# Tail scores of two heads moved from one full-array product into four quarter-array products, output weights rounded on chip, new order of work

## The chip, the cores and the metric

One core of a Trainium2 chip runs the whole program. The metric is device time in microseconds of one execution, as a median of runs; less is better. TensorE (PE, with its weight loads listed apart as PEld), VectorE (DVE), ScalarE (ACT) and GpSimd (POOL) compute, and the queue of SyncE (SP) issues nearly all DMAs.

## The reference

Two stages. First an attention with a window of 128 keys and a linear bias per head, over 8 batches, 8 heads, 576 positions, head size 64:

```python
scores = scale * q @ k.T
mask = (rel >= 0) & (rel < 128)
attn = softmax(where(mask, scores + bias, -1e9)); x = attn @ v
```

Then four experts of causal attention on x (8 x 576 x 512), the two best experts of each position weighted by their gate:

```python
w, topk = softmax of the 2 largest of x @ w_gate
for e in range(4):
    q, k, v = x @ wq[e], x @ wk[e], x @ wv[e]
    ye = causal_softmax(scale * q @ k.T) @ v @ wo[e]
    out += (weight of e in topk, else 0) * ye
```

## The kernel before

Two heads of a batch form a pair `g` (32 pairs, four in each batch). In SBUF the 64 dimensions of head 0 lie in partitions 0 to 63 and those of head 1 in 64 to 127. The 576 query rows of a head are four blocks of 128 and a tail of 64 rows. A block needs the keys of its own block and of the one ahead, the tail the last 192 keys.

Scores of the blocks (`products`) are fp32 products of 64x64 weights: each quarter of the PE array takes 64 rows of one head against 128 or 192 keys, and four such products, one in each quarter, stand together. `attn_s(g, 0)` makes blocks 0 and 1 of both heads (a group of four with 128 columns and one with 192), `attn_s(g, 1)` blocks 2 and 3 (two groups with 192). The tails of the two heads are the unit `attn_s(g, 2)`: one product over the whole array, whose 128x128 weights hold head 0's tail and zeros above, zeros and head 1's tail below, against 192 key columns, into a PSUM bank of its own. An fp32 product shows as two matmul records. Then DVE folds the late keys over the early ones (`copy_predicated`), adds the bias and takes the maximum, and ACT takes the exponential.

Inputs of a pair come in one SBUF slot `r` of the pool `big5`: `load` issues two DMAs of 288 KB (and the one of V), `load_hi` one of 64 KB with the tail's weights. `big5` has nine slots of 1280 floats; pairs' inputs, their probabilities, the experts' V and probabilities, and the raw weights share them. The first batch's four pairs go by another path (`half_s`, `half_tail`), with their own loads.

The output weights `wo` are needed rounded (`WOH`) and as a remainder (`WOL`). Before, `WOH` comes by a converting DMA that POOL issues, and POOL makes `WOL` from it and from the raw copy, which SP's queue loads.

Everything is recorded first, then issued in an order written out as a packed string (`ORDER`): each engine executes its instructions in that order, and SP's queue its DMAs. `plan` keeps the products of a quarter group together. Slots of a pool are given out along that order, the longest free first, so a load waits until the slot's last user is done. All instructions are issued by one line (L1185).

Of the kernel before, what the change touches and what calls it, by code (L numbers as in the profile page):

```python
# [34 lines left out]
K = {'nb': 0, 'm0': 8, 'm1': 0, 'he': 3, 'kj': 1, 'ot': 2, 'rn': 1, 'gr': 0, 'pw': 0.9, 'wa2': 0.9, 'q0': 0.1, 'q1': 1.0, 'wc': 3, 'se': 0, 'hd': 1, 'S': 2, 'T': 2, 'A': 2, 'X': 1, 'M': 1, 'apv': 0, 'alag': 2, 'vorder': 0, 'na': 1, 'pp': 3, 'tp': 6, 'mp': 3, 'ta0': 0.08, 'ta1': 0.91, 'sa0': 0.1, 'sa1': 1.0, 'sb0': 0.68, 'sb1': 0.77, 'tb0': -0.03, 'tb1': 1.08, 'wo0': 0.1, 'wo1': 0.45, 'wa0': 0.05, 'wa1': 1.3, 'aa0': 0.0, 'aa1': 1.04, 'ab0': -0.04, 'ab1': 1.0, 'xp': 5, 'ts': 1, 'lead': 0, 'na0': 2, 'wb0': 0.18, 'wb1': 1.0, 'sh': 0, 'man': 1, 'mode': 'rank', 'chn': 150, 'wu': 0, 'w0': 0.04, 'w1': 0.83, 'w3': 1.15, 'wd': 2}  # L35
# [7 lines left out]
    "b)oif*-BkgVLWqaFtT{ZkYf#(NCy06W%5K-#fYof}o*n4^`S<XhW%!bsPa1OM`AnL-(9}1W{_DSlTzz7$z8B<II(BY0qyt|HMgYT!%a9*#&*m*@yir6K"
    "Lr**f!ZR;Js7@N)4jsb-a8wM$yuLvgyw{zZ9(K8tOUH`~LUj{-X)2`Qc|>sJWm+A!wUmo;Z)xJ*cCoY6J!MO>nZT*dwSl)-_^|Cyr+GbSxF<jQ$LA|zn"
    "y9xZHo+pmt!<|jO2O+X*H!ZADFD*|cZp;8viPjLl>9;-(w+6WMPSAk*KT|7=v+BrAqzX&>wWTT<^CF9wI=TA&pn<dSel@*rLhIPdu;&zy=8z@|M7>!&Q"
    "Cj2>Y&vLTiUjc)&>Y#;RFUyXUCKQY>)(cy-w$blQQt!12{f{5O$IuuNBAs(I1M9UGMvJy*9%%b%AHoXF#Kl2cbbo<u(4w640b!2Vh?zfXOlZ$Z!{aGlB"
    "_+igy$ww?MshvTx9q|55(^TA{=gOam)MNom_xUl_}D4-PTU7n+4iVG^K)qClt7)m8g3s@k9Z&EGs~aBuw6<D$M^0KUPVrnl~%<`3GMfAL;^=#D4B?Q**"
    "o0P62eLN4&L&2E^_GU-iv2#(r9N0lKP#$b`Z+7E_OWBEmGjbCe=Ek?Dg%Y`nax>aEaR(Y#=zhH!)eFf~We6l>)x8j045|a+_1v1C8j27Z?6S<O<IyXNj"
    "7{j6U=IQzFEO5Z$0UQ#KWI{C=aPvpM{`Wte`{7lc2I+N1>&~d|(`?blKD@r}y&-DtX){7W+lZE5U|v{lZHfCu<LcziPF-Gp=()JM7W-to{XhTY`B!s-e"
    "6dNizxN><!v4_U?X5#j9=HH9^{INR!{x3XaYD=I9?2~7)Y-AyD*(L1Yu!S965pKyMx=+uRr`0pEoR*r61+Q}WP>L=v3;1LjN}e1ul8-O;s4HbXS&vqkv"  # L50
    "cnN>;@<(ZZ^^}8Tc;`Ix~6<7x5c40lvIsmCsH;Xh}@q+cWH@4iJQ^AKRUM{pIuN#&sAlJaWBLKMI|%{AuYFw9y%QCVTb81z&sd!~b;%b{cWk<ES<l(p%"
    "-kS}@?hUE|^1)wA4ha|UCN^CQpH1o_c{-o-8LxZtwg(maverhz8~bZ7tJB*FgNBzQ}vNBD}fb62s82dDM#f57~a4xxu?zLDk3;LUe(Nj|3`{OOiCVAAU"
# [20 lines left out]
    "1Fg1qJl%avzH;`n-de}r0{gDq`H2H<CKCn3rSc$E|V!-YaR{aoY#J$Os*D{?mJ%+b|{Q^ahZy4+grD;nHO|Fhmkgw1+&5LudX+FMmbX-=4#Zbx7`n*Yh"
    "5g)9v?wSn+d<IS$ScCMv>RqGd;l25nL~kJ`)V|sC#)jH9zCAFMRdW+6i%@pGj`<3ln-ZpGp})rt0VwY2M|DNG8K{{more;f0VArpd~v6z<rGf8|8U;=&"
    "B}XOWH&e>&`>)&g@c~IX*t<_^h>o3H`nz*wu7(20xjAw!p4E-=-S8AS3WB|eK4?f4WXSMj;%MgkBy!KKZcfOr-O?vsZCeEno(9dcDn<P92<3;cl`1Fw%"
    "mD7=J990l6FveL!3K@lN$>&sW`f3Ya@tQ3pBtf+}<^~ySFvGCAT+t8-~b|+_#g{@&T*=(f%x_p#6gn_64+P6D&yY0PU$YN66MJkU))K>cENB`O}wng>Y"
    "kKm$-fljPLq<%e{^^Ta9Z-$Py0ujWVnCROBaNA7Bss9aKZq;~%VkELbatPjPh)Ro$IVyuI5uNa|vsx?V?v9S?Ol7wQgD2e{Yq<3{%kJo54|<Ywj$XA-8"
# [1195 lines left out]
```

## Time and profile before

| | |
|---|---|
| time, median of 3 runs | 510.36 us (509.54 to 511.25) |
| profiled execution | 512.19 us, its span 510.4 us |
| granted PE clock | 0.997 of full speed |
| PE busy | 499.9 us (98%), 5044 matmuls |
| DVE, ACT, POOL busy | 418.6, 357.5, 171.6 us |
| DMA | 44.87 MB, mean 88 GB/s |

Times are in us unless marked ns. The span runs from the first to the last instruction of the profiled execution. Matmuls are pipelined, so durations of neighbouring matmuls overlap: the price of one in a stream is the distance from its start to the next one's, not its own duration.

### The profile page before, as it was taken

Reading aid. Unit: us, or ns where it says so; the run is one execution under the profiler, and the core shown is the slowest. Engines: PE = TensorE matmul, PEld = TensorE weight load, DVE = VectorE, ACT = ScalarE, POOL = GpSimd, SP = SyncE. Lnnn points to the kernel's source line nnn. Section 1 sums busy time; section 2 is a strip of 40 time slices with the busy share of each in tenths; the row PEclk is TensorE's granted clock in tenths of the full one; section 3 lists DMA queues with packets and bytes.
Section 4 is the critical chain, followed back from the end, with each engine's and each line's share of the span. In section 5 each row is a group of like instructions: output and inputs, shape, how many; then the busy total and the mean of one; then the engine's idle time right before and its main releaser. Section 6 shows DMA issues by size and latency. Waiting matters only on the chain.

```text
span 510.4 us, 14576 instructions
## 1 busy us (share of the span) xinstructions
PE 499.9 (98%) x5044; PEld 429.2 (84%) x5044; DVE 418.6 (82%) x1875; ACT 357.5 (70%) x1338; POOL 171.6 (34%) x382
## 2 busy tenths in 40 slices
...
GB/s 202 283 200 201 50 117 70 3 53 156 19 134 99 2 28 230 6 193 17 19 186 59 103 2 91 193 1 3 150 92 128 99 2 1 91 22 1 1 83 125
DMA packets 27307, 44.87 MB, mean 88 GB/s; under 512 B 3169, under 2 KB 11361, under 8 KB 27233
## 3 DMA queue, kind: packets, MB, share of 16 engines
q1 hardware_dynamic: 26352, 42.95, 31.2%
...
q10 hardware_dynamic: 736, 0.46, 0.3%
q0 software_dynamic: 144, 0.52, 0.3%
...
## 4 chain that ended last, share of the span: by engine, by line
PE 95%; DMA 3%; DVE 1%; ACT 0%; issue 0%; SPq 0%
PE ps L1185 95%; DMA w<-in_hd 3%; DVE w L1185 0%; ACT w L1185 0%; DVE ps L1185 0%; DVE r L1185 0%; DVE ps L1183 0%; DVE nmA L1185 0%; SPq L1185 0%
## 5 line engine op out<-in xcount | busy, mean ns | idle before, releaser
L1185 PE MATMUL ps<-wx,WH 128*128 128x288 f32 (+2 forms) x512 | 113.0, 301 | 0.0
L1185 ACT ACTIVATE w<-w,nm 128x128 f32<-128x128 f32 x252 | 98.6, 394 | 20.1 <-DVE nm L1185 19.9
L1185 POOL TENSOR_SCALAR w<-w,mr,w 128x256 f32<-128x256 f32 (+3 forms) x128 | 76.4, 607 | 91.2 <-DVE r L1185 28.7
L1185 ACT COPY w<-ps 128x512 f32<-128x512 f32 (+3 forms) x144 | 67.2, 491 | 38.4 <-PE ps L1185 28.7
L1185 POOL TENSOR_SCALAR w<-w,r 128x128 f32<-128x128 f32 x141 | 50.5, 370 | 121.9 <-DVE r L1185 89.0
L1185 PEld LDWEIGHTS ps<-wx,WH 128*128 128x128 f32 x512 | 83.8, 189 | 1.6 <-DVE mnm L1185 0.3
L1185 ACT ACTIVATE w<-w,mnm 128x128 f32<-128x128 f32 (+3 forms) x128 | 70.7, 554 | 18.5 <-DVE mnm L1185 18.4
L1185 PE MATMUL ps<-idt,w 128*128 128x128 f32 x608 | 80.3, 275 | 2.0 <-DVE nmA L1185 2.0
L1185 DVE CUSTOM_DVE_ANT_0 w<-ps,tbt 128x128 f32<-128x128 f32 x288 | 73.1, 284 | 4.8 <-PE ps L1185 2.6
L1185 PEld LDWEIGHTS ps<-idt,w 128*128 128x128 f32 x608 | 68.8, 141 | 7.0 <-ACT w L1185 2.7
L1185 DVE TENSOR_TENSOR w<-ps,tmt 128x512 f32<-128x512 f32 (+2 forms) x96 | 71.6, 771 | 3.6 <-ACT w L1185 2.1
L1185 PE MATMUL ps<-wx,WL 128*128 128x288 f32 (+2 forms) x256 | 72.0, 297 | 0.0
L1185 PE MATMUL ps<-w 64*64 64x192 f32 (+2 forms) x1088 | 63.2, 321 | 3.3 <-DMA w<-in_hd 3.3
L1185 PE MATMUL ps<-w,vt 128*64 128x256 f32 (+2 forms) x784 | 65.8, 308 | 0.0
L1185 PE MATMUL ps<-WH,wx 128*128 128x260 f32 x288 | 63.7, 289 | 0.0
L1185 PEld LDWEIGHTS ps<-w,vt 128*64 128x64 f32 x784 | 44.8, 137 | 19.6 <-issue 3.0
L1185 ACT ACTIVATE w<-w,r 128x128 f32<-128x128 f32 x147 | 52.1, 395 | 7.8 <-DVE r L1185 7.3
L1185 DVE COPY w<-ps 128x512 f32<-128x512 f32 (+3 forms) x78 | 43.1, 558 | 17.1 <-PE ps L1185 16.7
L1185 PEld LDWEIGHTS ps<-w 64*64 64x64 f32 (+1 forms) x1088 | 45.1, 139 | 13.7 <-issue 4.2
L1185 DVE COPY_PREDICATED ps<-mkt,ps 128x128 f32<-128x128 int32 (+2 forms) x160 | 50.0, 329 | 7.0 <-PE ps L1185 6.0
L1185 PE MATMUL ps<-w,w 128*64 128x64 f32 (+4 forms) x576 | 53.2, 319 | 0.0
L1185 DVE CUSTOM_DVE_ANT_0 w<-ps,mtt 128x384 f32<-128x384 f32 (+2 forms) x96 | 50.5, 550 | 1.7 <-PE ps L1185 1.3
...
## 6 DMA issues: line engine op xcount, KB each, us to landing
w<-in_hd SPq DMA_DIRECT2D x56, 288.0 KB, 5.1
...
```

The source lines that it names most:

```text
L1185: getattr(getattr(tc.nc, e), m)(*a, **k)
```

## The change

For the 28 pairs of the later batches, the tail's single product goes and four products take its place, one in each quarter, right behind the groups of `attn_s(g, 0)`: head 0's tail against key block 3 (128 columns), head 1's tail against key block 3 (128 columns), and each against the last 64 keys (64 columns). They write free columns of the two PSUM banks of that unit, and the tail's bias and exponential follow there; the unit `attn_s(g, 2)` is empty. The lower half of the array now needs head 1's tail and keys too, so `load_hi` issues three DMAs (32 KB in pieces of 256 bytes, 32 KB in pieces of 512, 16 KB in pieces of 256) in place of one of 64 KB, and the slots of `big5` grow to 1344 floats and fall from nine to eight; the pool `big2` has ten slots in place of nine. `WOH` is no longer loaded by the converting DMA: it is rounded from the raw copy by POOL or ACT. The order string is another: unpacked it has 5851 entries in place of 5795, 16 filler matmuls as before.

```diff
-K = {... 'wd': 2}
+K = {... 'wd': 0}
 ORDER = (
...
-    pp = big5 = _Slots(cp, 9, 10 * P, "w5")
+    pp = big5 = _Slots(cp, 8, 2 * S + 3 * D, "w5")
     tp = big10 = _Slots(cp, 4, 2 * (S + TAIL + S), "w10")
-    big2 = _Slots(cp, 9, DM, "w2")
+    big2 = _Slots(cp, 10, DM, "w2")
...
     def load(g):
-        r = big5.tile([P, 2 * S + P], F32, tag="r", name=f"r{g}")
+        r = big5.tile([P, 2 * S + 3 * D], F32, tag="r", name=f"r{g}")
...
     def load_hi(g):
         b, p = divmod(g, NP_)
         r, vt = loaded.pop(g)
-        nc.sync.dma_start(r[:, 2 * S :], hd[b, p, :, QW + S : QW + S + P])
-        k = r[:, S : 2 * S]
-        prepped[g] = (None, None, None, vt, (r[:, : NQ * P], k, r[:, 2 * S :], k[:, S - TW :]))
+        a = hd[b, p]
+        row = a.ap[0][0]
+        src = bass.AP(tensor=a.tensor, offset=a.offset + D * row + NQ * P, ap=[[row, D], [QW, 2], [1, TAIL]])
+        nc.sync.dma_start(r[D:, 2 * S : 2 * S + 2 * TAIL].rearrange("p (a n) -> p a n", a=2), src)
+        t = 2 * QW + S + P + (NQ - 1) * P
+        nc.sync.dma_start(r[:D, 2 * S + TAIL :], a[:D, t : t + P])
+        nc.sync.dma_start(r[:D, 2 * S : 2 * S + TAIL], a[:D, QW + S + P + TAIL : QW + S + 2 * P])
+        prepped[g] = (None, None, None, vt, r)
...
     def attn_s(g, u):
-        s = s_tile(g, u)
         if u == 2:
-            o = s[:, :TW]
-            nc.tensor.matmul(o, e[2], e[3], start=True, stop=True)
-            nc.vector.copy_predicated(s[:, 0:TAIL], mkt[:, P:], s[:, P:TW])
-            jobs = [(0, tbt[:, p, 4], -SCALE, 4)]
...
             return
+        ss = [s_tile(g, u), s_tile(g, u + 3)]
+        part = products(ss, 2 * u, [e[:, : NQ * P], e[:, TAIL:S]], e[:, S : 2 * S], tbt[:, p], 5)
+        if u == 0:
+            c = slice(3 * P, 4 * P)
+            lo, up = e[:D], e[D:]
+            x, m = 2 * S, S + (NQ - 1) * P
+            nc.tensor.matmul(ss[0][:D, c], lo[:, NQ * P : S], lo[:, m : m + P], start=True, stop=True)
+            nc.tensor.matmul(ss[0][D:, c], lo[:, x : x + TAIL], lo[:, x + TAIL :], start=True, stop=True)
+            c = slice(3 * P, 3 * P + TAIL)
+            nc.tensor.matmul(ss[1][:D, c], up[:, x : x + TAIL], up[:, x + TAIL : x + 2 * TAIL], start=True, stop=True)
+            nc.tensor.matmul(ss[1][D:, c], up[:, :TAIL], up[:, m + P :][:, :TAIL], start=True, stop=True)
+            nc.vector.copy_predicated(ss[0][:, c], mkt[:, P:], ss[1][:, c])
+            part[0].append((3 * P, tbt[:, p, 4], -SCALE, 4))
+        for h in range(2):
+            wrap(ss[h], 2 * u)
+            blocks(g, ss[h], part[h])
```

## Rows read from the trace of the kernel before

**Rows 1.** The page's first part: busy time of each engine.

```profile
PE 499.9 (98%) x5044; PEld 429.2 (84%) x5044; DVE 418.6 (82%) x1875; ACT 357.5 (70%) x1338; POOL 171.6 (34%) x382
```

**Rows 2.** Stretches: length, busy of PE, PEld, DVE, ACT, POOL, granted clock, DMA share, GB/s.

```profile
40.00:50.00 10.00, 8.17 (x93) 7.18 (x91) 8.86 (x38) 8.08 (x39) 1.76 (x5) 1.00 0.93 225
50.00:500.00 450.00, 449.57 (x4493) 387.04 (x4494) 373.75 (x1656) 319.26 (x1180) 151.19 (x346) 1.00 0.26 71
500.00:510.00 10.00, 6.59 (x74) 5.67 (x72) 2.81 (x7) 1.54 (x4) 0.00 (x0) 1.00 0.47 159
```

**Rows 3.** Waits of PE: total us, times, longest us.

```profile
PE ps L1185 <- DMA w<-in_hd: 3.3, 4, 2.3
```

**Rows 4.** The chain that ended last, in order of time: start, us, what.

```profile
34.43 9.18 DMA w<-in_hd
...
43.63 6.66 DMA w<-in_hd
...
50.43 456.17 PE ps L1185 x4555
```

**Rows 5.** Groups of matmuls kept apart by shape: busy us, mean ns.

```profile
L1185 PE MATMUL ps<-w 128*128 128x192 f32 x64 | 15.9, 339 | 0.0
...
L1185 PE MATMUL ps<-w 64*64 64x128 f32 x256 | 14.1, 282 | 1.1 <-DMA w<-in_hd 1.1
```

**Rows 6.** Timeline of PE around one tail product: start, us, instructions.

```profile
392.13 0.30 PE L1185 MATMUL ps<-wx,WL 128*128 128x288 f32 x1
392.27 0.49 PE L1185 MATMUL ps<-w 128*128 128x192 f32 x2
392.46 0.83 PE L1185 MATMUL ps<-wx,WH 128*128 128x288 f32 x4
393.12 0.29 PE L1185 MATMUL ps<-wx,WL 128*128 128x288 f32 x1
```

**Rows 7.** Timeline of PE: two runs of quarter products and what follows them.

```profile
189.50 0.88 PE L1185 MATMUL ps<-w 64*64 64x192 f32 x16
190.31 0.33 PE L1185 MATMUL ps<-idt,w 128*128 128x128 f32 x1
...
250.50 1.42 PE L1185 MATMUL ps<-w 64*64 64x192 f32 x32
251.85 0.50 PE L1185 MATMUL ps<-WOH,AHm 128*128 128x512 f32 x1
```

**Rows 8.** The page's DMA queues: packets, MB, share of 16 engines' span.

```profile
q1 hardware_dynamic: 26352, 42.95, 31.2%
...
q10 hardware_dynamic: 736, 0.46, 0.3%
q0 software_dynamic: 144, 0.52, 0.3%
```

**Rows 9.** DMA issues: count, KB each, median us to landing.

```profile
w<-in_hd SPq DMA_DIRECT2D x56, 288.0 KB, 5.1
...
WOH<-in_wo POOLq DMA_DIRECT2D x1, 512.0 KB, 9.1
```

**Rows 10.** Groups of POOL by shape: rounding and remainder of weights.

```profile
L1185 POOL TENSOR_SCALAR WH<-w 128x772 fp32r<-128x772 f32 x3 | 2.5, 847 | 0.3 <-DMA w<-in_wall 0.3
...
L1185 POOL TENSOR_TENSOR WOL<-w,WOH 128x1024 fp32r<-128x1024 f32 x1 | 2.4, 2411 | 0.0
```

**Rows 11.** Timeline of POOL: the DMA of the output weights.

```profile
32.61 0.75 POOL L1185 DMA_DIRECT2D WOH<-in_wo  x1
```

**Rows 12.** Timeline of PE: first use of the output weights, a later quarter run.

```profile
126.54 0.71 PE L1185 MATMUL ps<-WOH,AHm 128*128 128x512 f32 x2
...
369.74 1.42 PE L1185 MATMUL ps<-w 64*64 64x192 f32 x32
```

**Rows 13.** Timeline of SP's queue: the loads issued ahead of that run.

```profile
359.68 2.53 SPq L1185 DMA_DIRECT2D w<-in_hd  x4
```

**Rows 14.** Waits of SP's queue: total us, times, longest us.

```profile
SPq L1185 <- PE ps L1185: 245.8, 32, 32.9
```

More of the change, by code (lines that the diff above doesn't have):

```diff
@@ L43 @@
[L43 to L52, printed above, removed]
@@ L73 @@
[L73 to L77, printed above, removed]
@@ L113 @@
[L113 to L114 removed]
+    "c-obC4OAo7m1b4FD^<~|ZpoHnDG?qNix}AugDtXRjS|>EMjDG)$^jopAb|vCVJtFW!y0BG0Wa({4tOC0HXMTod0`C+%t8WVaOeciX%a|a3>$O;4xG@FW"
+    "*1_Z>7GDLC*8a3eN`$+V9%axb+@`ys`qp6{qA?a`xusqT#v=YKhAs$s>CEB0$iI}IOO3-m??rD`1-G*-Jk;p5i}M0hI)gj_w5Hw`dGa~V=!B0O`7@TPP"
+    "`ijvmb5;H3H!m4Cb%Crzg8z&J|<q8WG@gf1(NW4)gUj<^mWi;RyqU*Y3=T(<%A-oN;~kbRFcXzodS_tb<1yHNtoQ?sLJm<nMfm2!&<t!~>VcS4UDneEh"
@@ new lines @@
+    "$(cYXC$&FocJ?e6P_nQJqU4I2O({FfjeS0#V`i^tb@hKR7<F~rQR9!;$-O^(fO)tXMLkCJbFS{)Bv8bdV^M80&SPcQ!c=iD|?utP%H)GW+QSHa49r2|%"
+    "BWvdWi@@%Xnb!-wKJqVxw!OT_YgR2ElQ)qZaEB;BsZB33VcYTT6STbmv+d-p)GN4yYJ@6KY!)?`P1MqJ5^u(;*-Xnl5qv|=$U#8^b-)zmOs%^Qw63aUc"
+    "m6ZVVA|YY{cmd|X2w+G6YgVAY(n{t)FnD>NLkGHrEV6}@5A+W70@~dJFTSOHga5up5Rw3wazMr~?-a(mge>7+?lSnQD$Bb}8a_5X5k&r2gc6W10>Iq8Z"
+    "UzHrg{eRP4*ckaZ@&doVzCP*+wA6SgRW@(ZY+ea49J|-?x&U!{XOSe{&H{$R!iB(v>sn)pv4%NTT(p=A9+v{YaAW=7`%0Cj0H2g%|Pzu=Gc9uxsw^jvF"
+    "Sz~cr6w%@&>JOu_V790C#+{0deut3fJHmKackDW9XWDss8DITToLnean`4+Q#b+scoIY{?fYD(ev^X>W|X--Sa<t(3EMm#b)qD4yT~!(}kvNK)@zKjK~"
@@ new lines @@
+    "|FDArC7#+T-K;ySX@(z^MaLc3|nUtqJ#7Fo>r2mkNEfBk_3O=@}LZmXlQ+?(gs-m4W1zasA*6v6yzP00j6_xi}4Js24ufzf#y8SPx<=zRsxYgXs{d{?l"
+    "*ezf3k(^u63Tm_HzS#A%J7+kA>iaNnO#Ot9j*bkNEl?YE*)dJ`=+eaQR9|UOr47XUGUa^*x+|pQLgIl^=qn-hx&GuNdhCzR0P30;icXi>gUVsMNvLJ1J"
+    "sCNHo4c1oxw4hsr>&y6T4X4J>&e)O~p;i!n#d&M_h1!wi)a0_-cet^lQP9(cbwk8xF~$Z+BQZl04@tZ5_&<x)bq~Gsu9{7<Kihr(U*8l4-T&~9WEMdE!"
+    "-l54{pufoMelFA?T1EyrUoblD7dLF6ii=x_W&#z2rbZ;i-IA=QJZE@Ljb1H0ElJ92(?T^a<jjzV}B3MMh1$LeJ*RBIeGnh3Y71-;?uN=;+#>}lbN1r@X"
+    "l3Brd7>P$9Zanut9@&019D94p~=0ZUHPsKna83{HH6YCszmDfm3m6-23o<davfY8_?Ab(1xLClV@21bkIr&WThlKJ-B=D<;#~YX~i+nk=lb7zmi^9bov"
@@ new lines @@
+    "+YzEH3trr$g`+A`@EM$X>+tJJKc^2JYI7R!wSsgGLLp#es7w|v!c=dDNTnYiO+5c~4slOWh$3eJsfSV$%8Wc~bp`;OLdbD6j-Lq+9RKC8*Kk<?;H(KzA"
+    "eeljfInk`ODsd(+<v-%_d;_=QPqG9qB+#puPyARUlM~>hcqHT&VM?+v(NVo@8CtdBPxcKJIzIlEItj&h2unn2%K)q#ir1smif^~Li`oZ7b8HHwO!cFtp"
+    "aj|hp8gFBJyvTi<w;8JTy0({vn*1B~sg9z~Nr<Z~$<3xF-3HKG?j)dX&II2N|7EB5nP1)jvk#M_*V~*3J;O@~+&TKDVRWb$3fr{*_4Tj)zz%V%1>}?=a"
+    "W=y*?{j80fF^H#l@IWx7OTb6S94O_YI9WT0vUY`S>zMX>k@oP`4b{kWt*U|+Fz}~>5?HOF(vVSu6cVAMo()s-A+u&GtxX>KH15~T^4>j)n7kuGFvdc5q"
+    "|>kbPsWjON(#Y9&Y#AJ0=NqLFcS(dru0@*yI>~4iCzBaSYGcw&B*GnnOU|rYVH%a2F~khJ_|$Po3#-Pp3)G2@0FH>T|#ZMr2--laDP$CQ3sPCqYII2t>"
@@ new lines @@
+    "cPEa=8|Zs~@{z`zF`Ii$GaaB(Zay;Iogt#Vl({=*8CxN{7i?2I17zd|oK7rp6(rdC+RnVVaIGy}B2Stg9QmMa#ap?TUfH9G}8{jlEu%F93c`*qm2n4f<"
+    "ZK=k-Dzklj;-q#N{MgCXZjON)#+B|4zG1wuM2FbUv)jsM6xDuoOY_6jV^3_)gsA>1;lJgYk;1G&?7B@S1;rVYlVDaVObMTosn>D`(5?ABRhCP1M%Ix26"
+    "Zt&(9VlE}yi|#>gLFyyF`wx{5=kpsWBWSnJ1p#}`RA4@2Qe`<*0Qgf9u~dO8rx^KUO*6?pcC~Sa`nAMFi&pl7ubbM2YT9&v`9MP(3Ghq5_*A_IIX;Ct<"
+    "IRr(R2$Qc>j>M->&w@_zy$?eQieN0-@1I=xNLEW1+mjhSfU1`1<#~a!QVl>SY_89tp)o%v8m#XCBbwUCuH8(KH!&tPgp>U7xqRWYhasCs%bnfN;E!T{N"
+    "w^TJ>j9<bJU<Q&!S`M8b@ovY^iIMCth8uPRP1_cRw&(4uS(F#{#J>Z7q7fjnvgPw5_=H1uKm;X|KJ$Ky7=GYb>I~Ta7Lsu$R^&nXbpdOcBX+XzKN^kAA"
@@ new lines @@
+    "{ci^citTyLWu0>og+MfY9$o5PUfhGA$EwpJ4chX;oNu&RFJr4)GVf%O0W5EMH*!?Z#&@;rn;(ogSdApWqe@NI50D?Kf}XRdOsc`tombU|~_+pISgWoJO"
+    "zB~BicrEdtD#<g2NPQ8S+9E^fN7^5X2v0`~H%gMm;>iqJl4YFb}Hj7rFW_)F|8R}x)`gNOG6AN3nco5Ptt}ZdwyhB8-sbT=7-H52giC+5{fQK%UN%@op"
+    "p^MUg5c6vyZ}5n+>mEM^TYI~Z10ElA4|Z=D1aG`6)w5Z#>=Zhzw%&$n?GL_JSWx`_qvj3}uJ+7cS@~vzrv1i#Nz0Qj3Q+c&r=b<g=G1{^b7xDkXg|2N3"
+    "n;dx=$BR5O8Q@Z_R!BtE|r%hr+F7r1+tV=EF2yX&#;F#6mLGP)|@sEZJh1GbYGn#c5R{G-R(H?*Y;{}7!2djJag|iKZg-}^5%~H$%l%~jVV(GQ(ny(ES"
+    "d+kWIT@jr6*HYSdvj7ueLj#QeJ98o4_BN2e~^=JE%DnEA6Ln=MawCe(^tAaDQ`$Cuh3Jkw81|v7eN0*X<^`sxxnFl<P3}rlmAQm^DI;a1t+QD9O$(K(9"
@@ new lines @@
+    "e>${*xgi{o00D;nbCfPD9nYJWpnU0+>EA=Dy=b>X0U;HRWN(b9I>W%cHPkWm9ID5=~4w;C-4HTj8sovkP@55b9abA$RU1&blF-W$4)##&APWWHkT>Lj+"
+    "VQ=0{jYO4Jer5gWO&!N61ZDk-GU#AJxV+U7bo!g!bTGyUGcwF543Mah$#iFizU=^><w%3cIkU>gtO-iZx5VTprRT&0roWI&n3(ruHe)A&qXkjkYz4=qa"
+    "iDRHI$?F5}!8_l8#+7Xz@{FSQF~X;Q_Brtn@RL`qm)|=)u4wd}`EvEmU^AcHaq`J44v`mby!&UCsmT$z<A32fS6yKHWzI=REgVQymnI@+p#kQ~>}ez0C"
+    ";*vVA+Hg1iE-02f@ylp;)tERKK{d}dp#9n7_NO+lISoC*~k1i4p%>sypHA7)doIK$Og~pwK!9XSd(pwn@k4vqfW)Re4t7WV6z~XDny57DA~N23r)dG4~"
+    "rz|y;`7m*73i+GH73&$kI8pX45ijt9nJC^=$SRFM)7))cp2q-+2_3CUz=>s%NJklO?TOo<0v_idS)eFfKXkiQmQl{tXbAN8Zc+zM906hkgj@d;j~jqTl"
@@ new lines @@
+    "Pj|GhWA_tzuuezWlIvUX;xAd5fx_g}0kgF-`*ro6t;#-Cv|@%k%9i*C*uew_Gaw)VH!1;8m-3hktF-C{0qI5qKETiZFghTBo<r2%OU#(k#+b0yyNO6t^"
+    "(UQ@jOPGf_vu~STpwV8EkxMR?Ptu!F$yqMToG%;G%F(-9-{$t(kdNT;v4`E-?2h9!5y+kB;&5feZtuyIMV=D>+Nv?@_weV!Um}9Th)%y!}=)yJ>hM3|L"
+    "Fkd}3X|qncCZC*sdwJAj*4+Ao@V}e|f)-kY+B!ZDn89IPZPU>71hNe@)+MGCrfA@{cW)sVde<ElGX{T2xp{m@Xjs?^#*baanNJcxu*9{h|1*Z`x%W(Qj"
+    "eS_GPEm?N5H-WbDEY{h?Ss0(_3XoDN7l~T<KO<#bEKqZ6LJ!hD|n$)2ivWiE9)?l2k~+Fqq3t=?#!w=T>v0~evQQ@6Rh)J<2DNB2fp}x!r~ms7Wb-(?B"
+    "K|7mamO>jZDt8q!ha>=FZyr>50~+T0{EtpZ=?_P!Go@ka+A0tvF3QqQn+VG~F}_VnX8yjNr2XmUS~Ev}PEe`lL6_t+kgj!iJ%!ekztWgDYU`4-{7n(1~"
@@ new lines @@
+    "s~OCb!d1y_O|w>ih4<qZqwrJb8%7U(R8>4{i`Z5ciJD;;#h*do%-fhK%nI-=W##bzi)%B3`>feLzP$%H${nJ_UuF^xZFrX$b)@?R|JiIuPZgVnc_`0AI"
+    "h8ErlKpL6+QixXz_vBu>&!7{_Q2CIpKe=7eWqPJ+%Ryy`bX^!RA;rcFb67G9mqU<F~+SmtS8WGspgq3Bu8^i**eHXHGb5dG#i_h);1lV_WMxJ??4%i&%"
+    "ZQZPGuM~O4>u#vj{`$vlb^K(H$8CqSPG9O*-xmx<LFj>g-O9<*@Nd2xn5r+-lST066DeG^lx-QrXe-<uM&pY>Xqi}l;|jDGQ;JY$qSAbXOG1BQBV18e-"
+    "_(Ud3Y(m_pEL>HdEeGXudm9ou!Km(?!mT{*4-z#grYJpAFvjc6{Z*~CtGP3jKjO{O<*@s4|Vl5^++gni!O|xY2%Xc5u351w!y7K5$P=til5fK@KsJzP@"
+    "DSJPdgI$K67!a(AM3jMVeTim>$wVQFd-Y)@`_z-H)tRY;9m4OsF>+j3fz#=jwHDL5=A~uBi|kU(n@Sbd#F3)Q9ggXlKvvtU}(|J&${xG);>$q<g-Lbl!"
@@ new lines @@
+    "HCZZunW2FsYl^5Mm~pMB$%e?v?6{><Ng2^oBdBKq&R$#vRDB8oJ=iW^l479%Px5ltz8<|uwxgI(j|lsG<F*VE+9A~{*^T=%Z?tgyt+YxHHKe3$ZK7XG6"
+    "JC^eaWizm}_vtNIfj1AZOivs;~({Y_WO~;V7I{(yvTq#czA<K=9Eg0Cpp4W$^I3Gd(`V%<rrX?}u3;)xXUAmb8Z7qKa##b^W)Gz(!|G1`1fdcR*CQ)(Z"
+    "YdY{X%2;k6RJPFCaa;+#DfQR29UZjS!^^sdb#{K6O2|%F+{BUzZSA4g^|UR-CRhWt<&skGsoCqPsk7$0|J^rrbw~RFSFsMY^OUd*UwfQy{^#zeQ`57be"
+    "O0vg#Jqoe=a5t+W{6@P3B)DYQ?d%d-CVr6<-Ca;oC7{Lam==_iT;YkzT$Ge7Ct`wQsLw`e(J;Cb$GKY%D*jpz2Ic`)CQxu2M}(%M@^`T(T929gpGHu-1"
+    "mS@5Vamy(FW@HpPPTu6#MAsD-(oda9%41zh$A_A*Qvqdv<bX5afN`Xyzzb?*h@ehW8*B@_L)|;O$3&Fge1qF)<C!x&r+rnf)DR|5_2mQC~LL1Y2?SO~J"
@@ L115 @@
+    "hTMw3M)#}m;3s*B;0;SEZqmHJ_jLZ*^xJXI+2VF9u{MPexV*z;|#d~Csf$U%jYmV}KoHf-b!BqBHDhtkPQn3>pcqZ-D9EcWG73@T|^DzsH>sB}t!p`uv"
+    "+UC9}hN={c5r($J6MI?nl$u`tPvEhRf!YStrvUAyU{V@8J0MCWcrdG3DWdEGR5E5uqA^8^F#$)^>CM2PDi9{Vz$jVz96Q<>eiU`jkOWm++2xB_>Y)sw_"
+    "37-bYXD3p8SOPLJsaUBAm#|MEEB(Rpz(mA{iWdElR;8#Tp>|X5Q0NYbROlmZc(gs|n)Y*Qp8LQlsdALUM)!4!;~)|TmdGth2xTPHv9a=rojeM-h@h4gE"
+    "Kew<(@04wG^BCE-H)2*<n+awCXL~-Sy#lwx$KiQPxw$Q#AoMIlw*~XP&PVAKF}BaQRm5Yi$V<Z|8@OezC>F{"
 )
```

104 lines of the change are left out of this document (30 added, 74 removed).

## The prediction

> **What bounds the kernel.** I read the busy shares first. PE works 499.9 of 510.4 us, the next engine, DVE, 418.6 [rows 1]. A share is an average, so the windows come next: from 50 to 500 us PE is busy 449.57 of 450, at full clock, and what it idles lies ahead of 50 and behind 500 [rows 2]. The reader is to see two regimes. In the middle only PE work that is removed can shorten the kernel; there every wait of another engine is covered. At the start PE waits, and the waits say for what: 3.3 us in four waits for the loads of heads, the longest 2.3 [rows 3]. The chain of work agrees and gives the place: one load is issued at 34.43 and takes 9.18 us, the next is issued when it has landed and takes 6.66, and only at 50.43 does PE go on [rows 4]. That wait sits in the stretch from 40 to 50, where the DMA engines are busy 0.93 of the time [rows 2]: it is bandwidth or the order of the loads, not PE. At the end PE is busy 6.59 of 10 us [rows 2]; this is the last batch's output, which the change touches only through the order.
>
> **Tail product removed.** 64 records of 128x192 over the whole array are 32 tails [rows 5], two records each; four belong to the first batch's other path, 28 change. The duration of a record (339 ns) is no price, since neighbours overlap. The timeline gives it: a tail starts at 392.27, four products of 288 columns follow, the next start is 393.12, so the five take 0.85 [rows 6]. One product of 288 columns takes 0.135 to 0.14 from start to start (392.13 to 392.27). 0.85 - 4 x 0.135 = 0.31; I take 0.32. No switch of the array's form is saved, since the tail stands among other full-array products.
>
> **Quarter group added.** A run of 16 quarter records (two groups with 192 columns) lasts from 189.50 to 190.31, 0.81 us; a run of 32 (three groups with 192, one with 128) from 250.50 to 251.85, 1.35 us [rows 7]. If a run costs s to enter and leave, a group a with 192 columns and b with 128: s + 2a = 0.81, s + 3a + b = 1.35, so a + b = 0.54. Shared out by columns, a = 0.32 and b = 0.22, which leaves s = 0.16. That a equals the tail's price for the same 192 columns supports the share. The new group is as long as its longest products, 128 columns: I take 0.22, because its two shorter products sit in the other row half and run beside them. It is appended to a run that exists already, so s isn't paid again. Bounds: at most as long as a group with 192 columns, 0.32; no shorter than 128 columns, where an equal split by columns already puts it; allowing 0.01 for reading the timeline on either side, 0.21.
>
> So 0.32 - 0.22 = 0.10 a pair, 28 x 0.10 = 2.8 us off PE's path; bounds 0 and 28 x 0.11 = 3.1. DVE's fold and maximum and ACT's exponential of the tail stay as many and as long; they hang on the run's first bank in place of one of their own, and one bank less is claimed for each pair.
>
> **Output weights.** The converting DMA is 0.52 MB on the queue that took 0.3% of 16 engines' span [rows 8], 0.003 x 510.4 = 1.5 us of all the engines, and it is issued at 32.61 and takes 9.1 us to land [rows 9, 11], right in the congested stretch that the chain goes through. In its place comes a rounding with 1024 columns: POOL rounds 772 in 847 ns [rows 10], so 1.12 us. It is costed at nothing: POOL is busy 1.76 of 10 us there [rows 2], and PE first uses the weights at 126.54 [rows 12]. Were that cover gone, POOL's next normalisation would be 1.1 us late. The remainder (2.41 us [rows 10]) stays.
>
> **Loads.** Per pair 192 pieces of 256 bytes and 64 of 512 replace 128 of 512: 128 more. A piece on ACT's queue cost 0.003 x 510.4 x 16 / 736 = 33 ns of one engine, with 625 bytes on average; on SP's queue 0.312 x 510.4 x 16 / 26352 = 97 ns, with 1630 bytes [rows 8]. 128 x 33 to 97 ns over 16 engines is 0.3 to 0.8 us a pair. From 50 us on that is hidden: the DMA share is 0.26 [rows 2]. For the three pairs whose loads I count ahead of the wait at 50.43 it is 0.8 to 2.3 us, against the 1.5 saved. I take 33 ns, the nearer size: 0.8, a gain of 0.7 of the wait at 50.43. Bounds: the whole wait of 2.3 gone, or 0.8 more. SP issues 56 more loads in all, the 56 entries by which the order grew; outputs and V loads queued behind them come one issue later each, and SP waits 245.8 us for PE anyway [rows 14], so this is hidden too.
>
> The Trainium skill speaks against this part: "DMA: Bandwidth & Descriptors", section "Specifications", wants pieces of at least 512 bytes for full rate, below that a read and write-back is added. By that rule each small piece would cost like a larger one, and the sum would lie at the 97 ns end: no gain at the start, the time 1.5 us later than my sum. No row here has 256-byte loads alone.
>
> **The sum.** The profiled execution took 512.19, 1.8 more than its span of 510.4 and 1.8 more than the median, 510.36. 512.19 - 2.8 - 0.7 = 508.7 for an execution like it; on the median 510.36 - 3.5 = 506.9. The order string as a whole I cost at nothing: it has the same 16 fillers and must issue the same work; its risk is in the rivals.
>
> **Rivals.**
>
> 1. *The order or the group gives nothing back.* If the four quarter products take as long as a group with 192 columns, the tail's gain is 0 and the start's 0.7 remains: 509.7. For it: a short product beside a long one saves nothing, and the trace has no group of such a mixture. Against: groups with 128 columns, which fit b = 0.22, are in it [rows 5, 7].
>
> 2. *More runs.* Each separate run of quarter products costs s = 0.16 [rows 7]. If the new order splits work into 18 more runs, 18 x 0.16 = 2.9 eats the tail's gain: 509.8. Against it: the tail joins a run, and nothing in the change needs more. The Trainium skill, "TensorEngine Tiling (Array Packing)", section "Key Properties", says that changing the array's form drains it; the s of these runs agrees.
>
> 3. *Late loads: slower.* Eight slots in place of nine: a load waits for an earlier release. Place: the four loads issued at 359.68 over 2.53 us; with 5.1 to land [rows 9, 13] the last is there at 367.3, and the next quarter run starts at 369.74 [rows 12], so 2.4 us are spare. A slot that comes more than 2.4 us plus the present distance later stops PE. A late load costs 2.3 us today [rows 3]; two of them would eat the 3.5, and from three it is slower by more than noise: 506.9 + 3 x 2.3 = 513.8. For it: SP already waits 32 times for PE, up to 32.9 us [rows 14]. Against: seven batches ran with only one wait of that size, and the slots in question are released by products that PE does anyway.
>
> 4. *The start clears wholly.* The whole 2.3 goes, and the end, where 3.4 us are idle [rows 2], gives one: 510.36 - 2.8 - 2.3 - 1 = 504.3.
>
> **How the numbers follow.** Less than 0.3% (1.5 us) can't be told from no change; the three runs span 1.7. Forecast 0.50, its own range 505.3 to 508.4: 2.8 off with both ends of the start, 2.3 gained or 0.8 lost. Rival 1 0.13, rival 2 0.08, rival 3 0.16, rival 4 0.13. Faster: forecast and rival 4, 0.63. Same: rivals 1 and 2, 0.21. Slower: 0.16. The range runs from 503.5 (rival 4 with the tail's upper bound and the end 0.5 better) to 512 (rivals 1 and 2, with the loads' loss of 0.8 in place of the gain of 0.7 and one more microsecond of waits); outside it stand most of rival 3 and a little of rival 4, not quite 2 in 10.
>
> **What would show it.** The full-array groups with 192 columns fall from 64 records to 8; 64x128 records rise by 112 and 64x64 ones (112) appear. In the timeline a run of 24 quarter records (blocks 0 and 1 and the tail) should last near 0.16 + 0.32 + 2 x 0.22 = 0.92. PE's busy time falls by about 2.8, the wait near 50 us shrinks below 2.3, and from there to 500 PE has no visible gap. Wrong it would be if PE shows new waits for loads of heads between 50 and 500 (rival 3), if runs of quarter products become clearly more (rival 2), or if the start's wait grows although the converting DMA is gone (small pieces, or a slot).

## The result, and the profile after

The changed kernel took 505.06 us (median; 504.86 to 505.44) against 510.81 us for the kernel before on the same chip: a ratio of 0.989, 95% interval 0.9866 to 0.9914, that is 5.75 us less, with an interval of 4.4 to 6.8. The forecast was 506.9, 3.5 less, with a range of 503.5 to 512. The direction was right and the time lies in the range, but the gain was about 1.6 times the forecast.

The page's first part, and PE's waits (total us, times, longest us), of the kernel after:

```profile
PE 498.3 (99%) x5212; PEld 428.3 (85%) x5212; DVE 420.0 (83%) x1879; ACT 352.5 (70%) x1313; POOL 178.2 (35%) x403
```

```profile
PE ps L1194 <- DVE ps L1192: 1.3, 1, 1.3
PE ps L1194 <- DMA w<-in_hd: 0.2, 1, 0.2
```

PE's busy time fell by 1.6 us only, from 499.9 [rows 1], while the profiled execution became 6.75 us shorter (505.44 against 512.19, of which 1.4 is the distance of 512.19 from the median of 510.81): the busy time is no measure of the gain. The waits for loads of heads fell from 3.3 us in four [rows 3] to 0.2 in one. The stretches that answer to [rows 2], columns as there, and the last piece of the chain:

```profile
40.00:50.00 10.00, 10.00 (x144) 8.84 (x135) 9.90 (x45) 8.81 (x40) 3.10 (x9) 1.00 0.37 109
50.00:500.00 450.00, 449.91 (x4671) 388.30 (x4667) 376.33 (x1659) 315.25 (x1160) 157.09 (x364) 1.00 0.28 75
500.00:503.60 3.60, 0.00 (x0) 0.00 (x0) 0.37 (x1) 0.00 (x0) 0.00 (x0) 1.00 0.36 93
```

```profile
2.86 4.03 DMA w<-in_hd
6.92 493.00 PE ps L1194 x5121
```

The stretch from 40 to 50 us is full, where 1.83 us were idle, and its DMA share is 0.37 where it was 0.93. The chain no longer passes through two loads [rows 4]: from 6.92 to 499.9 it is PE alone. Read by itself that says "PE is the bound and nothing else"; the run with the doubled fold, below, shows what this reading misses.

The groups by shape (busy us, mean ns) and two runs of quarter products:

```profile
L1194 PE MATMUL ps<-w 64*64 64x128 f32 x368 | 26.1, 292 | 0.3 <-DMA w<-in_hd 0.2
...
L1194 PE MATMUL ps<-w 64*64 64x64 f32 x112 | 7.9, 217 | 0.0
```

```profile
136.53 0.98 PE L1194 MATMUL ps<-w 64*64 64x128 f32 x24
137.44 0.55 PE L1194 MATMUL ps<-idt,w 128*128 128x128 f32 x3
...
241.67 1.63 PE L1194 MATMUL ps<-w 64*64 64x128 f32 x40
243.22 0.55 PE L1194 MATMUL ps<-idt,MPL 128*128 128x128 f32 x3
```

The counts are as forecast: 64x128 rises from 256 [rows 5] by 112, 112 records of 64x64 appear, and 128x192 over the whole array falls from 64 to 8. (A run of mixed shapes is printed with the shape of its first record.) The run of 24 lasts 0.91 us, forecast 0.92. The run of 40 lasts 1.55 where the run of 32, the same run without the tail's group, lasted 1.35 [rows 7]: the group costs 0.20. Over all the runs of these two make-ups in the two traces the medians are 1.56 and 1.35, so 0.21.

POOL around the rounding (start, us), and the DMA side, queue and issues (count, KB each, median us to landing):

```profile
51.41 1.04 POOL L1194 TENSOR_SCALAR WOH<-w 128x1024 fp32r<-128x1024 f32 x1
52.43 0.24 POOL L1194 TENSOR_SCALAR QJm<-QLm 64x64 fp32r<-64x64 f32 x1
52.63 2.43 POOL L1194 TENSOR_TENSOR WOL<-w,WOH 128x1024 fp32r<-128x1024 f32 x1
```

```profile
q1 hardware_dynamic: 29040, 43.42, 31.8%
...
w<-in_hd SPq DMA_DIRECT2D x56, 288.0 KB, 4.5
...
w<-in_hd SPq DMA_DIRECT2D x56, 32.0 KB, 3.7
...
w<-in_hd SPq DMA_DIRECT2D x28, 16.0 KB, 3.7
```

```profile
SPq L1194 <- PE ps L1194: 220.7, 35, 23.1
```

The software queue of the converting DMA [rows 8] is gone, the large loads land in 4.5 us where they took 5.1 [rows 9], and SP waits no longer for PE than before [rows 14].

### The profile page after: what moved, and what is told of

It reads as the page before. It is cut to its first block, busy times and chain, and to the rows that moved or that the text cites. A ratio compares the mean times of both kernels' runs of the same rounds, so it can differ in the third digit from the quotient of the medians.

```text
span 503.6 us, 15006 instructions
## 1 busy us (share of the span) xinstructions
PE 498.3 (99%) x5212; PEld 428.3 (85%) x5212; DVE 420.0 (83%) x1879; ACT 352.5 (70%) x1313; POOL 178.2 (35%) x403
## 3 DMA queue, kind: packets, MB, share of 16 engines
q1 hardware_dynamic: 29040, 43.42, 31.8%
## 4 chain that ended last, share of the span: by engine, by line
PE 98%; DMA 1%; SPq 0%; DVE 0%; issue 0%
PE ps L1194 98%; DMA w<-in_hd 1%; SPq L1194 0%; DVE w L1194 0%
## 5 line engine op out<-in xcount | busy, mean ns | idle before, releaser
L1194 ACT COPY w<-ps 128x512 f32<-128x512 f32 (+3 forms) x132 | 62.4, 499 | 41.5 <-PE ps L1194 32.1
L1194 POOL TENSOR_SCALAR w<-w,r 128x128 f32<-128x128 f32 x156 | 55.9, 369 | 92.7 <-DVE r L1194 29.7
L1194 ACT ACTIVATE w<-w,mnm 128x256 f32<-128x256 f32 (+3 forms) x128 | 70.8, 555 | 15.1 <-DVE mnm L1194 9.5
L1194 DVE TENSOR_TENSOR w<-ps,tmt 128x1024 f32<-128x1024 f32 (+2 forms) x96 | 71.6, 772 | 2.6 <-PE ps L1194 1.3
L1194 DVE COPY w<-ps 128x256 f32<-128x256 f32 (+3 forms) x90 | 47.7, 544 | 18.8 <-PE ps L1194 18.1
L1194 PE MATMUL ps<-WH,wx 128*128 128x260 f32 x288 | 62.3, 284 | 0.0
L1194 PE MATMUL ps<-w 64*64 64x192 f32 (+2 forms) x1256 | 57.7, 313 | 0.3 <-DMA w<-in_hd 0.2
L1194 PE MATMUL ps<-w,w 128*64 128x64 f32 (+4 forms) x576 | 51.6, 318 | 0.0
L1194 DVE COPY_PREDICATED ps<-mkt,ps 128x256 f32<-128x256 int32 (+2 forms) x160 | 49.7, 329 | 1.1 <-PE ps L1194 0.5
L1194 ACT ACTIVATE w<-w,r 128x128 f32<-128x128 f32 x132 | 46.2, 395 | 5.3 <-DVE r L1194 5.1
```

Of the source, the lines that this page charges most:

```text
L1194: getattr(getattr(tc.nc, e), m)(*a, **k)
```

## The experiments

Two theories stood against each other. Theory A is the forecast's: in the middle of the kernel PE's work alone sets the pace, so the gain is the work that PE lost, plus a little at the start. Theory B: other engines, VectorE above all, are so close behind that with the order fixed only a part of PE's time comes back; the remade order carries much of the gain. Each expectation on record says what the theories give for its run, in the form that they had by then. Each run's ratio is to the kernel before on the same chip, with its 95% interval in brackets.

**The slots before.** The old order, with three slots instead of four for the transposed probabilities, was meant as a control for the runs that need that room.

```diff
-    tp = big10 = _Slots(cp, 4, 2 * (S + TAIL + S), "w10")
+    tp = big10 = _Slots(cp, 3, 2 * (S + TAIL + S), "w10")
```

> The kernel before with three slots in place of four for the transposed probabilities (never more than three are in use at once). A control for the two runs that need the room. Both theories: no difference from the kernel before, within 0.5 us of 510.8.

Measured: 510.28 us, 1.0007 [0.9977, 1.0037]. Its waits of PE:

```profile
PE ps L1183 <- DVE nmA L1183: 2.2, 1, 2.2
PE ps L1183 <- DMA w<-in_hd: 1.6, 4, 0.6
```

The slot costs nothing. The row says more: with the order of before the longest wait for a load is 0.6 us here, not 2.3 [rows 3]. The wait near 50 us, on which the forecast's term for the start stands, is not in every execution.

**The rounding alone.** The kernel before with `WOH` rounded by POOL right ahead of the remainder, no converting DMA.

```diff
-K = {... 'wd': 2}
+K = {... 'wd': 0}
 ORDER = (
...
```

> The kernel before with one edit: the output weights rounded by GpSimd right before their remainder is taken, no converting DMA. Theory A (that DMA's 0.52 MB makes the load before 50 us late): the wait of 2.3 us there shrinks by about 1.5, time 509.3. Theory B (the wait comes from where the loads stand in the order): wait as long as before, time 510.8.

Measured: 509.93 us, 0.998 [0.9959, 1.0002], that is 1.0 us less, between 2.1 less and 0.1 more. Its waits for loads of heads come to 0.9 us in three.

**The new parts in the old order.** Quarter group, loads and rounding, but the order of before: the group goes behind its pair's quarter run, and the tail's fold, maximum and exponential directly behind that run's fold. Nine slots of `big5`, three of `tp`.

> The tail as quarter products, the new loads and the rounding on chip, but with the old order of work (the quarter group set behind its pair's run, its fold and exponential behind that run's fold), nine slots kept. Theory A (the removed work and the removed converting DMA carry the gain): 28 x 0.11 = 3.1 off and about 0.7 at the start, 507.0. Theory B (the new order carries most of it): at most 1 us off, 510 or more. If A holds in part, what is missing to 505.1 is the order's share.

Measured: 538.07 us, 1.0537 [1.05, 1.0574]; both theories missed it by far. A second form kept the consumers at their old places in the order wherever these lie behind the products (8 of 28 pairs; the 20 others stay moved):

> The order of before with the tail product as a group of quarters behind its pair's quarter run, with the three loads and the rounding on chip; fold, maximum and exponential of the tail stay at their old places in 8 of 28 pairs and stand behind the quarter run's fold in the 20 others, where the old place lies ahead of the products. Theory A (TensorE's work alone): 28 x 0.115 = 3.2 us below before, 507.5. Theory B (the new order carries the gain, and the old one makes TensorE wait for folds and exponentials): no gain, above 511, up to the 538 of the run that moved the consumers of all 28 pairs.

Measured: 533.37 us, 1.0417 [1.038, 1.0453]. PE's waits in this second form:

```profile
PE ps L1191 <- ACT w L1191: 8.1, 5, 3.2
PE ps L1191 <- DMA w<-in_hd: 3.7, 3, 2.7
PE ps L1191 <- DVE nm L1191: 3.3, 5, 1.9
```

Less work on PE and 21 us more time (0.0417 x 510.8). PE now stands waiting for exponentials (ACT w) and maxima (DVE nm). So the new parts can't be had with the old order; how much a new order gains by itself, these two runs don't tell.

**The old tail in the new order.** The kernel after with the tail as two full-array products (128 and 64 columns) behind the quarter run, into the same two banks.

```diff
-            nc.tensor.matmul(ss[0][:D, c], lo[:, NQ * P : S], lo[:, m : m + P], start=True, stop=True)
-            nc.tensor.matmul(ss[0][D:, c], lo[:, x : x + TAIL], lo[:, x + TAIL :], start=True, stop=True)
+            nc.tensor.matmul(ss[0][:, c], e[:, x : x + P], e[:, m : m + P], start=True, stop=True)
...
-            nc.tensor.matmul(ss[1][:D, c], up[:, x : x + TAIL], up[:, x + TAIL : x + 2 * TAIL], start=True, stop=True)
-            nc.tensor.matmul(ss[1][D:, c], up[:, :TAIL], up[:, m + P :][:, :TAIL], start=True, stop=True)
+            nc.tensor.matmul(ss[1][:, c], e[:, x : x + P], e[:, m + P : m + P + TAIL], start=True, stop=True)
```

> The changed kernel with its order and slots, but each tail as two full-array products (128 and 64 columns, the same banks) behind the quarter run, and one load of 64 KB for it as before. Theory A: 28 x (0.32 - 0.21) = 3.1 slower than the changed kernel, 508.2, and up to 0.16 more for each of the tails that now stands between two other forms of the array (at most 21): 508.2 to 511.5. Theory B (the tail's form is worth nothing by itself): 505.1.

Measured: 520.66 us, 1.018 [1.0148, 1.0211]. One row of PE's timeline shows one reason why this is no price of the tail:

```profile
222.91 0.66 PE L1182 MATMUL ps<-w 128*128 128x128 f32 x4 [1.18 <-DVE nm L1182]
```

The product stands at a place where VectorE's work on the same banks is ahead of it, so PE waited 1.18 us for VectorE's maximum. Such waits come to 3.6 us in five, of about 15 us lost; the others were not traced. The run is inconclusive on the tail, and one more sign of how closely the two engines' orders are meshed.

**The group twice.** The kernel after, each quarter group of the tail issued two times; the order is the same.

```diff
+            for again in range(2):
...
+                c = slice(3 * P, 4 * P)
...
```

> The changed kernel with each tail's group of four quarter products issued twice in a row. Theory A (PE's work alone sets the time): 28 x 0.205 = 5.7 more than the changed kernel, 510.8. Theory B (the order and its waits set it): well under that, 505 to 507.

Measured: 510.76 us, 0.9997 [0.9977, 1.0017]. The distance to the kernel after is (0.9997 - 0.989) x 510.8 = 5.5 us (3.9 to 7.1, the two intervals taken together), 0.20 for each of 28 groups. In the timeline a run with the doubled group lasts 1.78 where the run of 40 lasts 1.56, so 28 x 0.22 = 6.0 were added. Work added to PE appears nearly in full.

**No tail products.** The same question from the other side: the kernel after, and the kernel before, without the tail's products (the tail's scores are left out; fold, maximum and exponential stay), in their own orders. Shown is the line that the kernel before loses; in the kernel after the four quarter products go in the same way.

```diff
-            nc.tensor.matmul(o, e[2], e[3], start=True, stop=True)
             nc.vector.copy_predicated(s[:, 0:TAIL], mkt[:, P:], s[:, P:TW])
```

> The changed kernel without the four quarter products of the 28 tails: the tails' scores are left out, what follows them reads what the bank held. Theory A: 5.7 less than the changed kernel, 499.3. Theory B: 503 to 505.

> The kernel before without the full-array product of the 28 tails: their scores are left out, what follows reads what the bank held. Theory A: 28 x 0.32 = 9.0 less than the kernel before, 501.4; then the difference to the changed kernel without its products (499.3) is what order, rounding and loads give, about 2. Theory B: 508 or more.

Measured: from after 502.46 us, 0.9837 [0.981, 0.9864], 2.7 less than after (0.9 to 4.6, the two intervals taken together) where 28 x 0.21 = 5.9 were taken from PE; from before 507.9 us, 0.9952 [0.992, 0.9984], 2.5 less (0.8 to 4.1) where 28 x 0.32 = 9.0 were taken. PE's first waits in the latter:

```profile
PE ps L1181 <- DVE nm L1181: 2.4, 3, 1.8
PE ps L1181 <- DVE nmA L1181: 1.7, 1, 1.7
PE ps L1181 <- DVE ps L1179: 1.3, 1, 1.3
```

Theory A falls here: work taken from PE came back to a half and to less than a third. The waits for VectorE that appear (nm, the maxima) are too short to be the whole of the missing 6.5 us; where such a rest can hide, the run with the doubled fold shows below.

This run also gives the price of a tail product. The stretch of [rows 6] without its tail:

```profile
387.13 0.30 PE L1181 MATMUL ps<-wx,WL 128*128 128x288 f32 x1
387.27 0.69 PE L1181 MATMUL ps<-wx,WH 128*128 128x288 f32 x4
387.79 0.30 PE L1181 MATMUL ps<-wx,WL 128*128 128x288 f32 x1
```

The two WL products are 0.66 us apart here and 0.99 in [rows 6], so this tail takes 0.33; the median over the places of all 28 tails is 0.32.

**A third of the tail product.** The kernel before with the product cut from 192 to 128 columns (the scores of the last 64 keys are left out).

```diff
-            nc.tensor.matmul(o, e[2], e[3], start=True, stop=True)
+            nc.tensor.matmul(s[:, :P], e[2], e[3][:, :P], start=True, stop=True)
```

> The kernel before, its order kept, with the tail product cut from 192 to 128 of its columns (the scores of the last 64 keys are left out): 28 products of TensorE become about 0.107 us shorter each, 3.0 us in all, while no other instruction is taken away. Theory A (TensorE alone sets the pace, so every microsecond taken from it comes back): 507.5 to 507.8 against 510.8. Theory B (VectorE and ScalarE are so close behind in a fixed order that only a third comes back, as when the whole tail product was taken out): 509.6 to 510.0.

Measured: 510.06 us, 0.9968 [0.9946, 0.999]: 1.6 less, between 0.5 and 2.8. Beside the kernel before, product by product, each tail is 0.10 us shorter (median), so 2.8 were taken and not 3.0. That is the end of the interval: the times alone don't rule theory A out here, the comparison at the end of this section does better. This is nearly the size of the change's own saving on PE, in the old order.

**Nine slots.** The kernel after with nine slots of pair operands instead of eight, and three of `tp`, to see whether loads come late.

```diff
-    pp = big5 = _Slots(cp, 8, 2 * S + 3 * D, "w5")
-    tp = big10 = _Slots(cp, 4, 2 * (S + TAIL + S), "w10")
+    pp = big5 = _Slots(cp, 9, 2 * S + 3 * D, "w5")
+    tp = big10 = _Slots(cp, 3, 2 * (S + TAIL + S), "w10")
```

> The changed kernel with nine of the large slots in place of eight (room made by three in place of four for the transposed probabilities). If the eighth slot makes loads late: less than 505.1 by the waits that PE shows for loads (0.2 us). If not: 505.1 within noise. Both theories expect the latter.

Measured: 506.53 us, 0.9913 [0.988, 0.9945], no better than with eight.

**The old start.** That kernel, with the first 370 entries of the order (about 34 us) as before and the rest as after.

> The kernel after with nine slots of pair operands, in which the first 370 entries of the order (about the first 34 us) are those of before and the rest is the new order. The kernel after with nine slots gave 506.5. Theory A (about 1 us of the order's gain lies in the first 20 us, where TensorE was busy 17 to 18 us with the new start and 15 to 16 us with the old one): 507.3 to 509.0. Theory B (the start is made up for later, since other waits stand behind it): 506.0 to 506.9.

Measured: 506.67 us, 0.9899 [0.9874, 0.9924], the same as with the new start. So no part of what the order gives is seen in the first 34 us; against the kernel after (0.989) the two intervals together leave room for 2 us.

**VectorE's fold twice.** The kernel after; VectorE folds the tail of each of the 28 pairs a second time, right behind the first. PE has nothing more to do.

```diff
+            nc.vector.copy_predicated(ss[0][:, c], mkt[:, P:], ss[1][:, c])
+            TIE.add(len(nc.ops))
             nc.vector.copy_predicated(ss[0][:, c], mkt[:, P:], ss[1][:, c])
```

> The kernel after, in which VectorE's fold of the 28 tails is done twice in a row (the second writes the same values again); nothing else is changed, the order too. One fold of this shape takes 0.29 us, so VectorE has 28 x 0.29 = 8.1 us more to do. Theory A (TensorE alone sets the pace, VectorE with 83% busy has room): 505.0 to 505.6, as the kernel after. Theory B (in a fixed order VectorE is so close behind TensorE that a third to two thirds of any time added to it appears in the span): 507.8 to 510.5.

Measured: 509.88 us, 0.9993 [0.9981, 1.0005]; (0.9993 - 0.989) x 510.8 = 5.3 us more than after (3.9 to 6.6). The fold's shape was mistaken in the expectation: it has 64 columns, and its group shows what was added,

```profile
L1194 DVE COPY_PREDICATED ps<-mkt,ps 128x64 f32<-128x64 int32 x32 | 7.1, 223 | 0.4 <-PE ps L1194 0.2
```

in the kernel after, and in this run

```profile
L1200 DVE COPY_PREDICATED ps<-mkt,ps 128x64 f32<-128x64 int32 x60 | 13.5, 226 | 2.0 <-PE ps L1200 0.8
```

so 6.4 us of VectorE's time, of which 5.3 came through: four fifths, by the interval three fifths to all, though VectorE is busy only 83%. Theory B holds, more strongly than it was put. Whether it is VectorE's throughput or the longer way from a pair's scores to its exponential, this run doesn't separate.

Where do these 5 us show? Here are this run's busy row and its waits of PE for VectorE:

```profile
PE 500.5 (98%) x5212; PEld 427.4 (84%) x5212; DVE 425.7 (84%) x1907; ACT 353.5 (70%) x1313; POOL 178.2 (35%) x403
```

```profile
PE ps L1200 <- DVE ps L1198: 1.3, 1, 1.3
PE ps L1200 <- DVE ps L1200: 0.9, 1, 0.9
PE ps L1200 <- DVE nm L1200: 0.5, 2, 0.3
```

PE still shows 98%, and the waits for VectorE grew by 1.4 us only. The timelines of the two kernels, beside each other, tell the rest. The kernel after:

```profile
37.94 0.28 PE L1194 MATMUL ps<-wx,WL 128*128 128x256 f32 x1
...
139.97 0.27 PE L1194 MATMUL ps<-idt,MPL 128*128 128x128 f32 x1
...
183.47 0.40 PE L1194 MATMUL ps<-WOL,AHm 128*128 128x512 f32 x1
183.70 0.47 PE L1194 MATMUL ps<-WOH,AHm 128*128 128x512 f32 x1
...
282.01 0.30 PE L1194 MATMUL ps<-wx,WL 128*128 128x288 f32 x1
```

The same products with the fold doubled:

```profile
38.32 0.28 PE L1200 MATMUL ps<-wx,WL 128*128 128x256 f32 x1
...
141.90 0.27 PE L1200 MATMUL ps<-idt,MPL 128*128 128x128 f32 x1
...
185.45 0.40 PE L1200 MATMUL ps<-WOL,AHm 128*128 128x512 f32 x1
186.17 0.50 PE L1200 MATMUL ps<-WOH,AHm 128*128 128x512 f32 x1 [0.33 <-DVE nm L1200]
...
285.56 0.30 PE L1200 MATMUL ps<-wx,WL 128*128 128x288 f32 x1
```

The lag grows slowly: 0.38 us at 38, 1.93 at 140, 1.98 and then 2.47 at 184, 3.55 at 282. It is made of many small stalls. One is caught in the rows: the second product starts 0.72 us after the first where it started 0.23 after it, a stall of 0.49, of which the trace counts 0.33 as idle. The record before is drawn 0.40 long although the next can start 0.23 after it; a stall shorter than that difference, 0.17 us, leaves no idle time at all. The Trainium skill's "Perfetto Trace Analysis", section "Tensor Engine Instruction (MATMUL, LD_WEIGHTS)", says that the end of a matmul's record is computed and not observed; these rows agree, and they show what it hides. The chain breaks at such places too. In the kernel after it was one piece of 493.00 us; here it is

```profile
192 pieces in order of time: start us, us, what
...
120.27 58.59 PE ps L1200 x591
186.17 141.47 PE ps L1200 x1445
```

**The middle by itself.** In traces of kernels with one and the same order the same product can be found again, so the stretch from about 52 us to PE's last product can be compared without the start. For the kernel before, and for the one with a third of the tail product cut, these rows bound it:

```profile
53.80 0.51 PE L1185 MATMUL ps<-WH,wx 128*128 128x260 f32 x2
...
506.32 0.27 PE L1185 MATMUL ps<-WOH,ALTm 128*128 128x256 f32 x1
```

```profile
52.59 0.52 PE L1182 MATMUL ps<-WH,wx 128*128 128x260 f32 x2
...
503.41 0.27 PE L1182 MATMUL ps<-WOH,ALTm 128*128 128x256 f32 x1
```

In the new order the first product is the transpose (`ps<-idt,w`, a run of nine) that starts at 51.43 us in the kernel after. Of the tails, 26 lie behind the first product in the old order and 25 in the new one. Times are in us:

| kernel | first | last | distance | put in (+) or taken out | change |
|---|---|---|---|---|---|
| before | 53.80 | 506.32 | 452.52 | | |
| before, three slots of `tp` | 51.60 | 504.02 | 452.42 | | -0.1 |
| before, rounding alone | 51.60 | 505.00 | 453.40 | POOL +1.0 | +0.9 |
| before, tail of 128 columns | 52.59 | 503.41 | 450.82 | PE 26 x 0.10 = 2.6 out | -1.7 |
| before, no tail products | 50.40 | 500.83 | 450.43 | PE 26 x 0.32 = 8.3 out | -2.1 |
| after | 51.43 | 499.63 | 448.20 | | |
| after, nine slots | 52.72 | 501.20 | 448.48 | | +0.3 |
| after, nine slots, old start | 51.98 | 500.01 | 448.03 | | -0.2 |
| after, group twice | 51.19 | 504.51 | 453.32 | PE +25 x 0.22 = 5.5 | +5.1 |
| after, no tail products | 51.27 | 497.28 | 446.01 | PE 25 x 0.21 = 5.3 out | -2.2 |
| after, fold twice | 52.15 | 504.56 | 452.41 | VectorE +25 x 0.23 = 5.8 | +4.2 |

These are single executions, but kernels whose engines have the same work agree within 0.3 us, far better than whole executions do: what these executions of one order differ in lies ahead of 52 us, and nothing of it is made up for behind. The rounding gives nothing in this stretch; what it may bring lies at the start. Of the work added to PE nine tenths appear, of that added to VectorE nearly three quarters; of the work taken from PE a quarter to two thirds come back.

## Why the prediction was right, and where its sizes were off

**The quarter group.** Right: 0.22 was forecast, 0.21 measured in the runs of 40 against 32 and 0.22 in the doubled group. A group of four unequal products is as long as its long ones; rival 1's mechanism is not there.

**The tail product.** Right: 0.32, by the kernel before with and without it. With the measured group the saving on PE is 28 x (0.32 - 0.21) = 3.1 us, for the 2.8 forecast.

**What bounds the middle.** The step that failed: "In the middle only PE work that is removed can shorten the kernel; there every wait of another engine is covered." Time added to VectorE came through by four fifths (5.3 of 6.4), and work taken from PE in a fixed order by a quarter to two thirds (2.5 of 9.0, 2.7 of 5.9, 1.6 of 2.8). PE's 449.57 of 450 us [rows 2] covers stalls that are shorter than the overlap of its records. In the old order 2.8 us off PE brought 1.6.

**The order, costed at nothing.** This is the mis-sized term. Under the new order the kernel carries 28 x 0.43 = 12.0 us of tail products (the group twice) in the time in which the old order carries 28 x 0.32 = 9.0, so new order, loads and rounding together are worth about 3 us (2 to 4 by that run's interval), against 0.7 forecast for rounding and loads. If the tail's 3.1 us came back in full, 2.6 of the 5.75 are left for the rest; at the price that removed work had in the old order (1.6 for 2.8) the tail has some 1.8 and the rest 4.0. So the gain is about 1.8 to 3.1 from the tail and 2.6 to 4.0 from the rest, of which the rounding alone has 1.0 (-0.1 to 2.1). These shares are found by subtraction, and the interval of 4.4 to 6.8 on the whole gain comes on top. It can't be split more finely, because neither part is had without the other: the old order with the new parts takes 533 to 538 us. The order's share is not seen in its first 34 us. By what rearrangement it comes, no run here shows.

**The start.** The wait for loads fell as forecast, but it can't be taken for the gain: in the other profiled executions with the old order it was 1.6 us (three slots), 0.9 (rounding alone), 0.2 (no tail products) and nothing (tail of 128 columns), and with the new one it was 1.5 in the kernel with the doubled group. The forecast took one execution's wait as the kernel's. It also left out what PE does ahead of 20 us. In the profiled execution of the kernel before PE idled about 3 us between 4 and 12 us, and the granted clock (the last column but two) then fell towards 0.5, the lower of its two levels, 1.2 GHz:

```profile
12.00:14.00 2.00, 1.98 (x8) 1.47 (x6) 1.71 (x12) 2.00 (x10) 0.83 (x3) 0.54 0.93 297
14.00:16.00 2.00, 2.00 (x33) 1.56 (x32) 0.96 (x4) 2.00 (x10) 1.74 (x2) 0.61 0.98 351
```

The kernel after shows 1.00 there. This is not the order's doing either: the new order with nine slots shows 0.67 and 0.50 in the same stretches, and the one with the old start 1.00.

**Loads.** Hidden, as forecast. The 128 additional pieces a pair are there: the DMA records have 5376 packets of 256 bytes where there were none, and 2304 of 512 bytes where there were 4096. (The queue's packets grew by 29040 - 26352 = 2688 only, since part of the large loads now goes in longer pieces.) Its time went from 31.2% of 510.4 to 31.8% of 503.6 us, by 0.9 us of all 16 engines; but that time is 158 to 161 us in the traces of before and its variants with the old loads, and 155 to 161 in those with the new ones, so no cost is seen, where 0.3 us a pair had been taken. A packet of 256 bytes took 21 ns on average, one of 512 bytes 35. The Trainium skill's "DMA: Bandwidth & Descriptors", section "Specifications", asks for pieces of at least 512 bytes; in this queue the pieces of 256 did not show the price that the forecast worked out from that rule, 0.8 us a pair at 97 ns for each of 128.

**Rivals 2 and 3.** The trace has 34 separate runs of quarter products where there were 31, three more, two of them in the first 16 us, and not 18. Late loads are not there: PE's waits for them are 0.2 us, and a ninth slot brings nothing. Output weights: POOL's rounding took 1.04 us, 1.12 forecast, at 51 us and far ahead of its first use.
